# Linear attention and a gated spatial unit on one core: x of the fourth batch turned by TensorE, variance offset and mean subtraction moved from VectorE into GpSimd's root and the normalization, and a new order table

## The chip, the cores and the metric

The kernel runs on one core of one Trainium2 chip. Its time is the device time of one execution in microseconds (us). A core has five engines with a queue each: TensorE (PE in the profile, its weight loads PEld), VectorE (DVE), ScalarE (ACT), GpSimd (POOL) and SyncE (SP), which here issues DMAs only. An instruction waits for semaphores of other engines at the head of its engine's queue, and whatever stands behind it waits too.

## The reference

Eight batches, eight heads, 576 tokens, head width 64. Attention is linear, with 128 random features:

```python
proj = np.einsum('bhsd,df->bhsf', x, w_phi)
proj = proj - np.max(np.abs(proj), axis=-1, keepdims=True)
phi  = np.concatenate([np.exp(proj), np.exp(-proj)], axis=-1)      # for q and for k
kv   = np.einsum('bhsf,bhsd->bhfd', k_p, v);  z = np.sum(k_p, axis=2)
attn = np.einsum('bhsf,bhfd->bhsd', q_p, kv) / (np.einsum('bhsf,bhf->bhs', q_p, z)[..., None] + 1e-06)
```

Its result, heads side by side, is x (8 x 576 x 512) of a gated unit:

```python
h = np.maximum(x @ w_in, 0.0);  u, v = h[..., :512], h[..., 512:]
v_n = (v - mu) / np.sqrt(var + 1e-06)                  # mean and variance over the 512
v_s = np.einsum('ts,bsd->btd', w_spatial, v_n) + b_spatial[None, :, None]
out = (u * v_s) @ w_out
```

## The kernel before, in words

Of each batch, 512 tokens are worked as four blocks of 128 (the main part); the last 64 tokens of two batches together make a fifth block (the tail, names with t at the end, one for each pair g of batches). Operands are bf16, sums fp32 in the eight banks of PSUM.

The work is cut into some 1400 small operations, each a Python function with a two or three letter name, and one long string, ORDER, lists them all in the order in which they are issued. A word `kp.0.1:2,3` is operation kp of batch 0, part 1, with buffers (or banks) 2 and 3; `@V`, `@A`, `@P`, `@S` names the engine of an operation that several engines can do: VectorE, ScalarE, GpSimd, SyncE. So the table decides three things: the order within each engine's queue, which engine does a copy or a normalization, and which buffer is used. Semaphores between engines follow from the buffers. An operation that is listed early on one engine can still run long before or after its neighbours in the list that are on other engines.

The stages of a batch b, with names:

- lk, lq: loads of k and q (from GpSimd's queue, with conversion to bf16); lv: v (from SP's queue). For the first batch's k, lkf and ckf load in quarters and convert on an engine.
- xk, xq: k and q turned by a transposing DMA on SP's queue; tk, tq with copies tkc, tqc: the same by TensorE and a copy, for the first batches.
- kp: projection of keys, km: largest magnitude (VectorE, L539), ke: the two exponentials (ScalarE, L543), kee and kem: exponentials of the maxima (L548). vs: v times these (L599), vsz: the column that gives z, vst and vstz: the same of the tail (L614). kv: the products of keys and values (TensorE, L634, and L636 with the tail's keys), kvc: copy of the result.
- qp, qm, qs, qt, qc: the same for queries, with the maxima split into two bf16 numbers (qs, L651 and L652), turned (qt) and copied (qc); qf: features with the maxima subtracted by matmuls (L660, L664), qe: exponentials (L669); qn: product with kv (L718), qr and qx: reciprocal (L724) and x (L731).
- x turned, into xT: by TensorE (tx, L801) and a copy (txc) for batches 0, 1 and 2, by a transposing DMA on SP's queue (xx, L794) for batches 3 to 7.
- vm: product with the v half of w_in (L833), vr: relu into vr; vb and va: statistics and aggregate on VectorE (L861, L867), which leave mean and variance in mv.
- vx and vy: add 1e-6 to the variance (L838), and negate the mean (L841), both in place on VectorE; vw: the root, GpSimd's power with exponent -0.5 (L844) into rs; vn: normalization, (vr + mv) * rs (L847), on VectorE or GpSimd. vbt, vat, vxt, vyt, vwt, vnt are the same for a tail.
- um and ur: the u half (L931) and its relu; sm: the spatial product (L946 with vn, L948 with the tail's vnt; smt, L992 and L994, gives the tail's tokens), sg: times u (L955); om: product with w_out (L960; omt, L1006, of the tail), oc: copy into ob, od: store.

The warm operations are matmuls on zeros (L334) in the gaps of the first stretch, whose results nobody reads. mv, rs and the banks are taken from small sets of buffers (six mv, five rs, three xT, three ld, four v).

The lines around the change:

```python
def prepare(mv):
    nc.vector.tensor_scalar(out=mv[:, :, 1], in0=mv[:, :, 1], scalar1=1e-6, scalar2=None, op0=ALU.add)
def negate(mv):
    nc.vector.tensor_scalar(out=mv[:, :, 0], in0=mv[:, :, 0], scalar1=-1.0, scalar2=None, op0=ALU.mult)
def root(rs, mv, r=slice(0, P)):
    nc.gpsimd.tensor_tensor(out=rs, in0=mv, in1=neghalf[r, 0:rs.shape[1]], op=ALU.pow)
def normalize(e, out_, in_, mv, rs):
    ENG[e].tensor_scalar(out=out_, in0=in_, scalar1=mv, scalar2=rs, op0=ALU.add, op1=ALU.mult)
```

Of the kernel before, what the change touches and what calls it, by code (L numbers as in the profile page):

```python
# [27 lines left out]
vs.0.1.1@P qt.0.1:3 qp.1.0.1:0,1 kem.0.2 vsz.0.2:3@P qc.0.1:1@V tqc.1.0.1:5@V vst.0.0.1@V vst.0.0.0@P vs.0.0.1@P
lv.0.1:1@S qst.0:2@P tq.1.0.0:4 qe.0.0.1.0:1 tqc.1.0.0@V qe.0.0.1.1 qf.0.1.1:2,3 qm.1.0.1:3 qe.0.1.1.1:2 kv.0.1:5
qe.0.1.1.0 qp.1.1.0:6,7 qm.1.1.0:0 vs.0.2.0@V kv.0.0:4 qf.0.1.0:0,1 vs.0.2.1@P qp.1.1.1:2,3 kvc.0.0:0@A kvc.0.1@A  # L30
qtt.0:4 qn.0.0.0:6,7 qct.0:2@A qe.0.1.0.0:3 qm.1.1.1 tk.1.0.1:4 kv.0.2:5 tkc.1.0.1:6@V qp.1.0.0:2,3 vs.0.3.0@P
kvc.0.2@A vs.0.3.1@P vst.0.1.0@P qe.0.1.0.1 tk.1.0.0:4 vst.0.1.1@P qr.0.0.0:0 kv.0.3:5 qx.0.0.0:0 qm.1.0.0 tkc.1.0.0@V
kvc.0.3@A lkt.1:0@S qft.0:6,7 lqt.1:1@S ckt.1:0@P qs.1.0:2@P qn.0.0.1:0,1 qr.0.0.1:1 qn.0.1.0:2,3 qx.0.0.1 qr.0.1.0:2
lv.1.0:2@S kp.1.1:4,5 qet.0.1:4 qx.0.1.0:1 qet.0.0 qn.0.1.1:0,1 qr.0.1.1:0 qnt.0.0:6,7 qx.0.1.1 tk.1.1.1:2 lv.1.1:3@S
ke.1.1.1:4 lk.2:2 qrt.0.0:1 tx.0.2:3 tq.2.0.0:0 tkc.1.1.1:0@V tx.0.1:1 tk.1.1.0:2 qxt.0.0:0 ke.1.1.0 txc.0.2:0@A
kp.1.0:6,7 tx.0.0:3 km.1.1:3 txc.0.1@A tkc.1.1.0@V tx.0.3:1 qt.1.0:4 txc.0.0@V qc.1.0:0@V vm.0.2:5 txc.0.3@V
tqc.2.0.0:1@V ke.1.0.0:1 ke.1.0.1 txt.0.0:4 qs.1.1:2@P vr.0.2:0@A lbs:0@S kp.1.3:2,3 ke.1.3.1:0 lq.3:1 kp.1.2:0,1
# [20 lines left out]
vb.1.2:0 qp.3.0.0:4,5 qe.2.0.0.0:4 sm.0.1:0 sm.0.2:1 qe.2.1.1.1:0 qe.2.1.1.0 qm.3.0.0 vs.2.1.0@P qe.2.0.0.1 sg.0.1
kp.3.0:4,5 qf.2.0.1:6,7 sg.0.2 va.1.0:2 vs.2.2.0@P qe.2.0.1.0:2 qp.3.1.1:0,1 zmhl.0@V km.3.0:0 kv.2.2:2 qm.3.1.1
vs.2.3.1:3@P vs.2.3.0@P xq.4.0:0@S vs.2.1.1@P qe.2.0.1.1 lv.4.0:3@S vsz.2.3@P lv.4.1:2@S vst.1.1.0@P um.1.0:3  # L60
qp.4.0.0:6,7 vsz.2.0:2@P kvc.2.2:2@A kp.3.1:0,1 ke.3.0.1:0 um.1.3:2 qs.3.1:2@P ur.1.0@V vs.2.0.0@P qst.1:0@P
xq.4.1:1@S ke.3.0.0 sm.0.0:3 qtt.1:4 km.3.1 qm.4.0.0:1 qct.1:0@V kv.2.1:5 ur.1.3@A ke.3.1.1:3 kee.3.0:0 qt.3.1:2
xk.4.0:3@S kv.2.3:4 sg.0.0 kp.3.3:6,7 qc.3.1:2@V kvc.2.1@A vbt.0.1:2 ke.3.1.0 kvc.2.3@A kp.3.2:2,3 om.0.0:5 km.3.3:2
ke.3.2.1:2 vs.2.0.1@P oc.0.0:0@V qs.3.0:0@P vsz.3.1:1@P ke.3.3.1:1 om.0.2:4 qt.3.0:0 vb.1.1:1 qc.3.0:1@V km.3.2
ke.3.3.0 kv.2.0:1 kvc.2.0@A om.0.3:5 oc.0.3:1@V vsz.3.0:0@P xk.4.1:5@S smt.0.0:0 oc.0.2:2@A sgt.0.0 qp.4.1.0:6,7
qf.3.0.0:4,5 qm.4.1.0:2 qn.2.0.1:0,1 qr.2.0.1:1 qx.2.0.1:1 ke.3.2.0 qn.2.1.0:2,3 qe.3.0.0.1:3 lk.5:0 qe.3.0.0.0
vs.3.0.1@P vst.1.1.1@P vs.3.1.0@P qft.1:6,7 vs.3.0.0@P qr.2.1.0:2 qn.2.0.0:0,1 lq.5:1 qn.2.1.1:4,5 qx.2.1.0:0
qet.1.0:2 om.0.1:2 qet.1.1 qr.2.0.0:0 ckt.2:0@P va.1.1 qx.2.0.0 od.0.0@S qr.2.1.1:1 vat.0.1:3 tx.2.1:3 lv.3.1:0@S
txc.2.1:2@A va.1.2 kee.3.1:1 oc.0.1:3@A vxt.0.1@V lk.6:2 vwt.0.1:2@P qp.4.1.1:0,1 qf.3.0.1:6,7 vyt.0.1@V qx.2.1.1
qm.4.1.1 qp.4.0.1:4,5 xk.5.0:4@S kv.3.0:3 tx.2.2:2 qe.3.0.1.0:1 tkt.2:0 vm.2.1:1 va.1.3 qm.4.0.1 qe.3.0.1.1 vnt.0.1@P  # L70
vr.2.1:2@A qf.3.1.0:4,5 kvc.3.0:0@V tktc.2:0@V vy.1.2@V kp.4.0:6,7 vx.1.2@V txc.2.2@V xk.5.1:2@S tx.2.3:3 vs.3.1.1@P
qe.3.1.0.0:4 kv.3.1:0 ke.4.0.1:4 tx.2.0:1 txc.2.3@V vb.2.1:1 kvc.3.1@A vm.2.2:2 qs.4.0:2@P qe.3.1.0.1 vsz.3.2:3@P
vw.1.2:3@P txc.2.0@V vm.2.0:3 vn.1.0:2@P va.2.1:4 km.4.0:3 vn.1.3@P vn.1.1@V qf.3.1.1:0,1 vn.1.2@P vr.2.2:1@A
kp.4.2:4,5 vs.3.2.1@P vsz.3.3:2@P sm.1.0:2 lvt.2:0@S vr.2.0:4@V sm.1.2:3 od.0.3@S km.4.2:1 vs.3.2.0@P vb.2.2:2
ke.4.0.0 qe.3.1.1.0:0 um.2.1:6 sg.1.0 smt.0.1:7 ke.4.2.1:0 sg.1.2 ke.4.2.0 qe.3.1.1.1 ur.2.1:0@V kp.4.1:2,3 vs.3.3.0@P
lqt.2:1@S kp.4.3:4,5 qs.4.1:0@P vb.2.0:0 vs.3.3.1@P sgt.0.1 kv.3.3:6 km.4.3 ke.4.1.1:3 kv.3.2:0 kvc.3.3@A kvc.3.2@A
# [75 lines left out]
def kernel(  # L152
# [684 lines left out]
    def prepare(mv):  # L837
        nc.vector.tensor_scalar(out=mv[:, :, 1], in0=mv[:, :, 1], scalar1=1e-6, scalar2=None, op0=ALU.add)  # L838

    def negate(mv):  # L840
        nc.vector.tensor_scalar(out=mv[:, :, 0], in0=mv[:, :, 0], scalar1=-1.0, scalar2=None, op0=ALU.mult)  # L841
# [214 lines left out]
```

## Time and profile before

| | |
|---|---|
| median of three runs | 260.94 us (259.86 to 262.88) |
| the profiled execution | 262.09 us, its span 260.3 us |
| TensorE busy | 243.9 us, 94% of the span |
| VectorE busy | 227.4 us, 87% |
| ScalarE busy | 193.2 us, 74% |
| GpSimd busy | 149.7 us, 58% |
| DMA | 40.79 MB moved, mean 157 GB/s |

How to read the profile's lines. A row of the windows holds a stretch of the span in us, its length, and for PE, PEld, DVE, ACT and POOL the busy time and, in brackets, the number of instructions; then the granted clock of TensorE as a share of full speed, the busy share of the DMA engines and the GB/s moved. A row of the timeline begins with start and duration in us, then the engine, the line of the code, the operation, what it writes and reads by the program's names with the shapes, and the count of instructions drawn together; in square brackets stands how long the engine was idle before it and what ended that. A row of the groups has the line, the engine and the operation, then busy time and mean ns of one instruction, then the idle time before the group's instructions and what ended most of it. The chain of waits is followed back from the last instruction: each step goes to what released it. A matmul's record reaches from its start to its modelled end, and one starts before the last has ended, so a busy TensorE need not be a full one.

### The profile page before, as it was taken

The numbers are of one execution on the slowest core, as the hardware profiler recorded it, in microseconds if no ns is written. First come the engines' busy times: TensorE is split into PE (matmuls) and PEld (weight loads), VectorE is DVE, ScalarE is ACT, GpSimd is POOL, SyncE is SP. The second block draws the span as 40 slices with busy tenths as digits, with TensorE's granted clock in tenths as the row PEclk, the third lists the DMA queues.
The fourth block names the chain that finished last, engine by engine and source line by source line (L and its number), as shares of the span: only waits on it lengthen the run. The fifth ranks groups of instructions, "written<-read, shape, count | busy, mean of one in ns | idle before, by whom it ended". The sixth has DMA issues, their size and how long they took to land.

```text
span 260.3 us, 8002 instructions
## 1 busy us (share of the span) xinstructions
PE 243.9 (94%) x3250; PEld 150.4 (58%) x3287; DVE 227.4 (87%) x427; ACT 193.2 (74%) x298; POOL 149.7 (58%) x235
## 2 busy tenths in 40 slices
...
GB/s 147 245 234 192 220 221 183 183 236 218 157 156 199 207 113 117 186 179 236 127 183 183 118 226 189 159 144 167 0 83 22 63 86 79 78 123 43 168 195 201
DMA packets 77767, 40.79 MB, mean 157 GB/s; under 512 B 46754, under 2 KB 72994, under 8 KB 77732
## 3 DMA queue, kind: packets, MB, share of 16 engines
...
q14 instruction: 10, 0.08, 0.2%
...
## 4 chain that ended last, share of the span: by engine, by line
PE 53%; DVE 26%; issue 9%; DMA 6%; ACT 2%; POOL 2%; POOLq 0%; DVEq 0%; ACTq 0%
PE banks L833 8%; PE banks L931 6%; PE banks L946 6%; DVE mq L539 6%; PE banks L634 5%; PE banks L960 5%; PE banks L534 5%; DVE mk L539 4%; PE banks L718 3%; DVE x L731 3%; DMA xT<-x 3%; PE banks L660 2%; DVE uT L955 2%; PE banks L664 2%; DMA T<-ld 2%
## 5 line engine op out<-in xcount | busy, mean ns | idle before, releaser
L669 ACT ACTIVATE qf<-banks 128x1024 bf16<-128x1024 f32 x72 | 70.2, 1035 | 6.8 <-PE banks L664 6.2
L599 POOL TENSOR_TENSOR vs<-v,em 128x512 bf16<-128x512 f32 x59 | 62.9, 1080 | 9.7 <-ACT em L548 9.4
L543 ACT ACTIVATE kf<-banks 128x1024 bf16<-128x1024 f32 x64 | 63.8, 1038 | 5.6 <-PE banks L534 4.6
L539 DVE TENSOR_REDUCE mk<-banks 128x8 f32<-128x1024 f32 x36 | 43.5, 1212 | 1.5 <-ACT kf L543 1.0
L539 DVE TENSOR_REDUCE mq<-banks 128x8 f32<-128x1024 f32 x36 | 43.1, 1211 | 0.5 <-PE banks L534 0.4
L844 POOL TENSOR_TENSOR rs<-mv,neghalf 128x4 f32<-128x4 f32 (+2 forms) x13 | 11.0, 844 | 52.6 <-DVE mv L838 50.5
L833 PE MATMUL banks<-w_v,xT 128*128 128x512 bf16 x115 | 30.6, 379 | 3.0 <-DMA xT<-x 2.2
L946 PE MATMUL banks<-w_spT,vn 128*128 128x512 bf16 x118 | 31.9, 379 | 0.5
L931 PE MATMUL banks<-xT,w_u 128*128 128x512 bf16 x128 | 32.3, 380 | 0.1
L960 PE MATMUL banks<-w_out,uT 128*128 128x512 bf16 x118 | 30.9, 379 | 0.6 <-issue 0.2
L255 ACT COPY ob<-banks 128x512 f32<-128x512 f32 x24 | 14.0, 589 | 21.6 <-PE banks L960 10.2
L534 PE MATMUL banks<-wphi,T 64*128 64x128 bf16 x512 | 23.7, 217 | 1.6 <-DVE mq L539 0.9
L955 DVE TENSOR_TENSOR uT<-banks,uT 128x512 bf16<-128x512 f32 x32 | 21.1, 678 | 4.1 <-PE banks L948 2.9
L634 PE MATMUL banks<-vs,kf 128*128 128x66 bf16 x512 | 23.9, 194 | 0.6 <-DVE vs L599 0.4
L634 PEld LDWEIGHTS <-kf 128*128 128x128 bf16 x512 | 21.5, 97 | 3.4 <-issue 0.5
L731 DVE TENSOR_TENSOR x<-banks,rc 128x512 bf16<-128x512 f32 x32 | 22.0, 686 | 0.8
L718 PEld LDWEIGHTS <-qf 128*128 128x128 bf16 x512 | 19.1, 97 | 4.5 <-issue 0.2
L861 DVE BATCH_NORM_STATS2 st<-vr 128x6 f32<-128x512 bf16 x32 | 21.3, 678 | 0.1
L636 PE MATMUL banks<-vst,kft 128*128 128x66 bf16 x128 | 21.1, 192 | 0.0
L534 PEld LDWEIGHTS <-T 64*128 64x128 bf16 x512 | 15.8, 94 | 8.9 <-issue 6.0
L718 PE MATMUL banks<-kv,qf 128*128 128x66 bf16 x512 | 20.4, 193 | 0.3 <-DVE x L731 0.3
L261 ACT ACTIVATE vr<-banks 128x512 bf16<-128x512 f32 (+1 forms) x21 | 12.8, 608 | 9.8 <-PE banks L833 9.5
...
## 6 DMA issues: line engine op xcount, KB each, us to landing
...
```

Of the source, the lines that this page charges most:

```text
L534: nc.tensor.matmul(out=bank(banks[y])[:, n * F:(n + 1) * F], lhsT=xT[halves[y], n, :], rhs=wphi[halves[y], :], start=True, stop=True)
L539: nc.vector.tensor_reduce(out=out_, in_=pp.rearrange("p y (n f) -> p y n f", f=F), axis=AX.X, op=ALU.max, apply_absolute_value=True)
L543: nc.scalar.activation(out=kf[:, s].rearrange("p y n f -> p y (n f)"), in_=pp, func=AF.Exp, bias=0.0, scale=(1.0, -1.0)[s])
L599: ENG[e].tensor_tensor(out=at["vs", (b, j)][:, s, :, 0:D], in0=at["v", (b, j // 2)][:, (j % 2) * n:(j % 2 + 1) * n, :], in1=at["em", (b, j ...
L634: nc.tensor.matmul(out=pv[:, hh, s, :], lhsT=kf[:, s, c % 2, 2 * hh + c // 2, :], rhs=w[:, s, NB * hh + c, :], start=(c == 0), stop=False)
L669: nc.scalar.activation(out=at["qf", u][:, s].rearrange("p y n t -> p y (n t)"), in_=at["pq", u], func=AF.Exp, bias=0.0, scale=(1.0, -1.0)[s])
L718: nc.tensor.matmul(out=at["pn", u][:, y, n, :], lhsT=f[:, s, y, n, :], rhs=at["kv", b][:, hg * HH + n, s, :], start=(s == 0), stop=(s == 1))
L731: nc.vector.tensor_tensor(out=at["x", (b, cc)][:, :, hg * HH:(hg + 1) * HH, :], in0=at["pn", u][:, :, :, 0:D], in1=at["rc", u].to_broadcas ...
L833: nc.tensor.matmul(out=bank(place)[r], lhsT=lhs[:, kc, r], rhs=w_v[:, kc, :], start=(kc == 0), stop=(kc == KC - 1))
L931: nc.tensor.matmul(out=bank(place).rearrange("p (c t) -> p c t", c=NB), lhsT=w_u[:, kc, dc * P:(dc + 1) * P], rhs=at["xT", b][:, :, kc, :] ...
L946: nc.tensor.matmul(out=bank(place), lhsT=at["vn", b][:, c, cs], rhs=w_spT[:, c, 0:T0], start=(c == 0), stop=False)
L960: nc.tensor.matmul(out=bank(place), lhsT=at["uT", b][:, dc, c * P:(c + 1) * P], rhs=w_out[:, dc, :], start=(dc == 0), stop=(dc == KC - 1))
```

## The change

Three things change together.

1. The operations vx, vy, vxt and vyt are gone, 26 instructions on VectorE. The root gets an addition of 1e-6 to the variance in place, on GpSimd, ahead of its power; the normalization subtracts the mean instead of adding its negative.

2. x of batch 3 is turned by TensorE (tx.3.0 to tx.3.3, four transposes each, with copies txc.3.0 on ScalarE and txc.3.1 to txc.3.3 on VectorE) instead of by xx.3.0 and xx.3.1, two transposing DMAs.

3. The table is a new one throughout: order, engines and buffers. Some counts of operations by engine, before and after: vs on VectorE 5 and 2 (GpSimd 59 and 62); vst on VectorE 2 and 0; vn on VectorE 8 and 4, on GpSimd 24 and 28; vnt on VectorE 2 and 0; ur on VectorE 14 and 9, on ScalarE 18 and 23; vr on VectorE 15 and 17; kvc on VectorE 11 and 17, on ScalarE 21 and 15; qc and qct on VectorE 16 and 7, on ScalarE 4 and 13. One of the first batch's four key conversions moves from VectorE to GpSimd, and one constant's two copies (zvnt.0) from VectorE to ScalarE. The matmuls on zeros grow from 29 to 33. The first loads are queued differently: of the four key quarters of batch 0, two are issued from SP's and two from ScalarE's queue as before, but all four ahead of any tail load, and the load of batch 1's q (lq.1) follows the first q loads directly on GpSimd's queue.

The core of the diff:

```diff
-    def prepare(mv):
-        nc.vector.tensor_scalar(out=mv[:, :, 1], in0=mv[:, :, 1], scalar1=1e-6, scalar2=None, op0=ALU.add)
-
-    def negate(mv):
-        nc.vector.tensor_scalar(out=mv[:, :, 0], in0=mv[:, :, 0], scalar1=-1.0, scalar2=None, op0=ALU.mult)
-
     def root(rs, mv, r=slice(0, P)):
+        nc.gpsimd.tensor_scalar(out=mv, in0=mv, scalar1=1e-6, scalar2=None, op0=ALU.add)
         nc.gpsimd.tensor_tensor(out=rs, in0=mv, in1=neghalf[r, 0:rs.shape[1]], op=ALU.pow)
 
     def normalize(e, out_, in_, mv, rs):
-        ENG[e].tensor_scalar(out=out_, in0=in_, scalar1=mv, scalar2=rs, op0=ALU.add, op1=ALU.mult)
+        ENG[e].tensor_scalar(out=out_, in0=in_, scalar1=mv, scalar2=rs, op0=ALU.subtract, op1=ALU.mult)
...
-    @op
-    def vx(e, b, i):
-        prepare(at["mv", b][:, spans[i]])
-
-    @op
-    def vy(e, b, i):
-        negate(at["mv", b][:, spans[i]])
...
-    @op
-    def vxt(e, g, i):
-        prepare(at["mv", ("t", g, i)][rows[i], 0:1, :])
-
-    @op
-    def vyt(e, g, i):
-        negate(at["mv", ("t", g, i)][rows[i], 0:1, :])
```

And the first lines of the table, before and after:

```diff
-zsp@V zvst.0@V cident@P lkf.1:0@A zmhl.2@V csel@V lkf.0:1@S zvnt.0@V ckf.1:0@V ckf.0@V lq0.4.4:1 lphi@A cphi@V
-warm.10:0 tk.0.0.1:0 lkf.3:2@A tkc.0.0.1:0@V lq0.0.4 tk.0.0.0:1 tkc.0.0.0@A ckf.3@P lkt.0:0@S csel2@V warm.1:2
-kp.0.1:2,3 warm.1:4 kp.0.0:4,5 ke.0.0.0:0 km.0.1:0 warm.8:6 tq.0.1.0:0 ke.0.1.1:1 km.0.0 tk.0.1.1:1 lkf.2:3@S lq.1:2
+zsp@V lkf.1:0@S zvst.0@V zmhl.2@V cident@P ckf.1:0@V lphi@A lq0.0.4:1 lq0.4.4 lkf.3:1@A lkf.2:2@A zvnt.0@A warm.8:0
+tk.0.0.1:0 csel@V csel2@V cphi@V tkc.0.0.1:0@A warm.4:1 kp.0.1:2,3 lkf.0:3@S lq.1:2 ckf.3@P warm.5:1 tk.0.1.1:0
+km.0.1:0 ckf.0@P kem.0.1:0 warm.1:1 tk.0.0.0:1 ckf.2@P tkc.0.1.1:1@V tkc.0.0.0@V kp.0.3:4,5 warm.1:6 kp.0.0:6,7
```

More of the change, by code (lines that the diff above doesn't have):

```diff
@@ L28 @@
[L28 to L37, printed above, removed]
@@ L58 @@
[L58 to L67, printed above, removed]
@@ L68 @@
[L68 to L76, printed above, removed]
-qt.4.0:1 qc.4.0:0@V vm.2.3:7 xq.5.0:6@S qnt.1.2:0,1 sm.1.1:6 km.4.1 ke.4.3.1:1 ke.4.3.0 ke.4.1.0 vr.2.3:3@A
@@ new lines @@
+kvc.0.0@A qn.0.1.0:6,7 qm.1.1.1 qr.0.1.0:0 ke.1.1.1:4 qx.0.1.0:0 qct.0:2@A ke.1.1.0 vs.0.3.0@P vs.0.3.1@P qs.1.1:2@P
+kv.0.2:3 kvc.0.2@A qft.0:0,1 km.1.1:3 qet.0.0:4 kv.0.3:2 qt.1.1:3 lv.2.1:0@S qc.1.1:0@A kvc.0.3@V qn.0.0.0:6,7
+qr.0.0.0:1 qx.0.0.0:1 qet.0.1 kp.1.0:4,5 lqt.1:1@S vst.0.1.0@P qn.0.1.1:2,3 ke.1.0.0:2 qr.0.1.1:2 qx.0.1.1
+qn.0.0.1:0,1 qr.0.0.1:0 qnt.0.0:6,7 ke.1.0.1 tx.0.3:2 qx.0.0.1 qrt.0.0:1 qs.1.0:2@P txc.0.3:0@A qt.1.0:3 qc.1.0:1@V
+qxt.0.0:0 tq.2.0.0:0 km.1.0 tq.2.1.1:1 tqc.2.0.0:1@A tq.2.0.1:3 kp.1.2:6,7 tqc.2.0.1@A tx.0.0:0 txt.0.0:2 txtc.0.0:0@V
@@ new lines @@
+sm.0.2:6 qf.2.1.0:2,3 qf.2.0.0:0,1 sg.0.2 vs.2.1.1@P ur.1.2:2@A vb.1.1:0 vs.2.3.1:3@P qp.4.1.0:4,5 qe.2.1.0.0:1
+qe.2.0.0.0:2 vsz.2.3@P qe.2.1.0.1 qe.2.0.0.1 vs.2.3.0@P qm.4.1.0:3 qs.3.1:1@P vsz.2.0@P lq.5:1 vs.2.2.1:2@P kv.2.1:6
+va.1.1 vb.1.3:2 sm.0.1:7 sg.0.1 kv.2.3:4 kvc.2.1:2@V kvc.2.3@A vb.1.0:3 um.1.1:5 vs.2.2.0@P qp.3.0.0:2,3 ur.1.1@A
+qm.3.0.0 vst.1.1.1@P xq.4.1:3@S kp.3.1:6,7 lqt.2:0@S kp.3.0:0,1 ke.3.1.1:0 km.3.0:1 lv.5.1:2@S ke.3.1.0 km.3.1
+vs.2.0.0@P vsz.2.2@P um.1.0:4 ur.1.0@A sm.0.3:5 kv.2.0:2 kvc.2.0@V kv.2.2:4 ke.3.0.0:1 va.1.3 kp.3.3:6,7 lkt.2:1@S
@@ new lines @@
+qp.4.0.1:0,1 oc.0.1:2@A um.1.3:3 qe.3.0.1.0:3 km.3.2 qm.4.0.1:2 tx.2.0:2 vst.1.1.0@P tx.2.1:4 qtt.1:5 qp.4.1.1:0,1
+qe.3.0.1.1 qct.1:0@V kee.3.1:2 ur.1.3@A vsz.3.0@P txc.2.1@V vn.1.0@P qft.1:6,7 vn.1.1@P vsz.3.1@P txc.2.0@A vn.1.2@P
+qm.4.1.1 qet.1.1:1 qet.1.0 qp.4.0.0:4,5 qm.4.0.0 smt.0.0:3 vm.2.2:2 sgt.0.0 qf.3.0.0:0,1 vsz.3.2:1@P kp.4.0:4,5
+vr.2.2:3@V km.4.0:2 vm.2.1:3 vr.2.1:1@V tx.2.3:2 qe.3.0.0.1:0 qe.3.0.0.0 sm.1.1:6 txc.2.3@V sg.1.1 qs.4.1:1@P
+ke.4.0.1:4 kv.3.0:7 qf.3.1.0:0,1 kvc.3.0:0@V lv.3.1:1@S vs.3.2.1@P kp.4.2:2,3 kp.4.1:6,7 ke.4.0.0 qe.3.1.0.0:4
@@ new lines @@
+tqtc.2:0@A vs.4.1.0:2@P qr.3.0.1:0 ur.2.2@A vs.4.2.0@P lk.6:1 qx.3.0.1 va.2.2 vst.2.0.1:0@P kp.5.0:0,1 kp.5.1:2,3
+vstz.2@P ke.5.1.1:3 vmt.1.2:6 vst.2.0.0@P vrt.1.2:0@A tx.3.2:7 qm.5.0.1 vw.2.2:4@P tx.3.3:4 kv.4.0:5 vn.2.2:0@P
+om.1.2:6 km.5.0:0 ke.5.1.0 txc.3.3:0@V txc.3.2@V vbt.1.2:1 kvc.4.0:1@A xq.6.0:5@S od.0.2@S oc.1.2:0@V tx.3.1:7
+ke.5.0.0:4 vsz.4.1@P xq.6.1:4@S vn.2.0@P om.1.3:4 ke.5.0.1 vat.1.2:5 km.5.1 vs.4.1.1@P vwt.1.2:1@P tx.3.0:5 qs.5.0:1@P
+vm.3.2:6 ckt.3:0@P qpt.2:0,1 lq.7:2 txc.3.0@A oc.1.3:1@A qf.4.0.1:2,3 qp.5.1.1:4,5 txc.3.1@V qe.4.0.1.1:4 qe.4.0.1.0
@@ new lines @@
+um.3.0:7 qmt.2:3 vr.3.2:3@V qt.5.0:0 vm.3.0:1 qm.5.1.1 vsz.4.3@P kee.5.0:2 vr.3.0:2@A qc.5.0:2@A kv.4.1:6 vst.2.1.1@P
+vn.2.1@P kvc.4.1@A kp.5.2:2,3 ur.3.0:1@V qp.6.1.0:4,5 qm.6.1.0:2 kp.5.3:0,1 ke.5.3.1:1 km.5.2:2 ke.5.3.0 km.5.3
+um.3.3:6 vs.4.2.1@P kv.4.2:7 um.2.1:4 kvc.4.2@V vm.3.3:5 ur.3.3@A kv.4.3:6 xk.6.1:3@S ke.5.2.0:2 vn.2.3@P odt.0@S
+lv.6.1:3@S xk.6.0:1@S vr.3.3:1@A kee.5.1:0 qn.4.0.0:0,1 qr.4.0.0:1 vs.5.0.0:3@P kvc.4.3@A vst.2.1.0@P um.3.2:5
+qf.4.1.0:6,7 vb.3.3:0 ke.5.2.1 qx.4.0.0:1 qp.6.1.1:2,3 qm.6.1.1 qn.4.0.1:0,1 qr.4.0.1:2 qx.4.0.1 vnt.1.2:0@P ur.2.1@A
```

189 lines of the change are left out of this document (96 added, 93 removed).

## The prediction

> **What bounds the kernel now.** I read the windows first, because the two halves of this program have different limits, then the timeline around the one stretch where every engine pauses, then the groups of lines for the durations. The windows give, per stretch, its length and then the busy time of PE, PEld, DVE, ACT and POOL.
>
> ```profile
> span 260.3 us, 8002 instructions
> 0.00:20.00 20.00, 15.59 (x158) 8.58 (x160) 16.82 (x28) 13.91 (x24) 11.59 (x27) 0.96 1.08 209
> 20.00:40.00 20.00, 18.63 (x338) 13.85 (x336) 19.23 (x36) 18.20 (x29) 14.82 (x22) 0.95 1.22 206
> 40.00:100.00 60.00, 59.17 (x913) 39.03 (x923) 58.99 (x112) 58.46 (x92) 49.01 (x77) 1.00 1.17 183
> 100.00:125.00 25.00, 21.35 (x308) 12.81 (x311) 22.03 (x39) 19.60 (x31) 19.18 (x29) 1.00 1.25 193
> 125.00:200.00 75.00, 73.59 (x1047) 46.20 (x1058) 70.82 (x128) 64.20 (x98) 45.74 (x72) 1.00 0.65 131
> 200.00:256.40 56.40, 55.60 (x498) 29.95 (x502) 39.51 (x90) 18.30 (x30) 9.38 (x11) 1.00 0.42 109
> ```
>
> From 40 to 100 us VectorE and ScalarE are both full (58.99 and 58.46 of 60): two bounds side by side, so relief of one alone is worth little there. From 125 to 200 us ScalarE has 10.8 us to spare and VectorE only 4.2, so VectorE is the tighter of the two. From 200 us on only TensorE is full. Its matmuls overlap, so "busy" is no measure of a dense queue; the last product is: 20 matmuls of 512 columns in 4.48 us, about 0.22 us each, with no gap, and the rows ahead of it join without gaps too.
>
> ```profile
> 249.91 1.03 PE L931 MATMUL banks<-xT,w_u 128*128 128x512 bf16 x4
> 250.78 1.03 PE L946 MATMUL banks<-w_spT,vn 128*128 128x512 bf16 x4
> 251.86 4.48 PE L960 MATMUL banks<-w_out,uT 128*128 128x512 bf16 x20
> ```
>
> So after 200 us an engine other than TensorE gains nothing; all that can be won is won before.
>
> One place loses time on all engines. The chain of waits holds the transposing DMA of batch 3 for 7.40 us, and the timeline shows three engines idle at its end: TensorE 2.23 us, VectorE 2.24, ScalarE 3.01.
>
> ```profile
> 114.53 7.40 DMA xT<-x
> 121.97 1.04 PE L833 MATMUL banks<-w_v,xT 128*128 128x512 bf16 x4 [2.23 <-DMA xT<-x]
> 123.12 0.69 DVE L263 TENSOR_SCALAR vr<-banks 128x512 bf16<-128x512 f32 x1 [2.24 <-PE banks L833]
> 123.38 1.94 ACT L543 ACTIVATE kf<-banks 128x1024 bf16<-128x1024 f32 x2 [3.01 <-PE banks L534]
> ```
>
> **The change part by part.** These rows price it (busy time, then mean ns of one).
>
> ```profile
> L838 DVE TENSOR_SCALAR mv<-mv 128x4 f32<-128x4 f32 (+2 forms) x13 | 1.9, 149 | 0.1
> L841 DVE TENSOR_SCALAR mv<-mv 128x4 f32<-128x4 f32 (+2 forms) x13 | 2.8, 215 | 0.1
> L599 POOL TENSOR_TENSOR vs<-v,em 128x512 bf16<-128x512 f32 x59 | 62.9, 1080 | 9.7 <-ACT em L548 9.4
> L599 DVE TENSOR_TENSOR vs<-v,em 128x512 bf16<-128x512 f32 x5 | 5.1, 1028 | 0.0
> L614 POOL TENSOR_TENSOR vst<-vt,em 64x512 bf16<-64x512 f32 x14 | 14.4, 1038 | 2.4 <-ACT em L548 1.9
> L847 POOL TENSOR_SCALAR vn<-vr,mv,rs 128x512 bf16<-128x512 bf16 x24 | 19.1, 804 | 0.6
> L847 DVE TENSOR_SCALAR vn<-vr,mv,rs 128x512 bf16<-128x512 bf16 x8 | 4.1, 525 | 1.4 <-POOL rs L844 1.4
> L847 DVE TENSOR_SCALAR vnt<-vr,mv,rs 64x512 bf16<-64x512 bf16 x4 | 1.6, 408 | 0.6 <-POOL rs L844 0.6
> L652 POOL TENSOR_TENSOR mhl<-mq,mhl 128x16 bf16<-128x16 f32 (+1 forms) x20 | 4.3, 215 | 1.6
> L844 POOL TENSOR_TENSOR rs<-mv,neghalf 128x4 f32<-128x4 f32 (+2 forms) x13 | 11.0, 844 | 52.6 <-DVE mv L838 50.5
> L263 DVE TENSOR_SCALAR uT<-banks 128x512 bf16<-128x512 f32 x14 | 9.5, 681 | 1.0 <-PE banks L931 1.0
> L257 DVE CAST kv<-banks 128x264 bf16<-128x264 f32 x11 | 4.6, 416 | 0.9 <-PE banks L636 0.9
> L261 ACT ACTIVATE uT<-banks 128x512 bf16<-128x512 f32 x18 | 11.0, 612 | 7.4 <-PE banks L931 7.4
> L255 ACT CAST kv<-banks 128x264 bf16<-128x264 f32 x21 | 8.1, 393 | 2.1 <-PE banks L636 1.9
> L543 ACT ACTIVATE kf<-banks 128x1024 bf16<-128x1024 f32 x64 | 63.8, 1038 | 5.6 <-PE banks L534 4.6
> 58.96 0.83 PE banks L801 x12
> ```
>
> Offset and negation: 13 times 0.149 and 13 times 0.215 leave VectorE, 4.7 us. GpSimd gets 13 additions on at most 128x4 numbers; no row shows that operation, the nearest small ones are 0.215 (L652) and, above, the power at 0.844, so 2.8 us, with bounds of 2.8 and 11.0. The normalization's subtraction is costed as the addition it replaces (0.804 on GpSimd), with the slower two-operand product (1.080) as the other bound, 0.3 us more for each of 28.
>
> The new table moves much more. Counting each operation's engine in the two tables: 3 vs, 2 vst, 4 vn and 2 vnt (two instructions each) go from VectorE to GpSimd, 3.1 + 1.9 + 2.1 + 1.6 = 8.7 us off VectorE. Between VectorE and ScalarE, five ur (0.681) and nine qc and qct go to ScalarE, six kvc (0.416) and two vr come back; netted (on ScalarE a ur is 0.612, a kvc 0.393) and with the turned blocks of the start counted the same way, VectorE loses some 1.6 us more and ScalarE gains 3.8. So VectorE loses 15 us in all, ScalarE gains 4 and GpSimd some 15 (11.6 for the products and normalizations, 2.8, and one conversion).
>
> Transposes of batch 3: 16 more on TensorE, by the L801 row 0.07 us each, 1.1 us, and four copies (three VectorE, one ScalarE); two DMAs leave SP's queue, behind which stood loads and other transposes.
>
> What lies on the path, stretch by stretch:
>
> - To 50 us: ahead of the last x of batch 0 the new table puts about 3 us more on ScalarE (three more key exponentials at 1.038; a constant's copies and two mT against two kvc about cancel), and ahead of batch 1's last key product four more GpSimd operations (a vs, a vst, a conversion, a load's issue), 3.6 us. In the trace these key products follow directly on GpSimd's products, but GpSimd sat 3.94 us idle shortly before, so most is covered. Against that, the key loads of the start are issued earlier, the fourth from ScalarE's queue instead of behind a tail's load. I take +0.9; bounds -1.5 and +3.5.
> - 50 to 100: VectorE has 3 to 4 us less at equal progress, ScalarE the same, so only the idle time that one makes for the other can go. ScalarE's is 1.5 of 60 us and VectorE's 1.0. I take -0.8; bounds 0 and -2.0.
> - 100 to 125: the wait on xT goes, -2.2. What is late next are the kp and qp of the following batches, also behind DMAs; bounds 0 and -3.0. The 1.1 us of transposes fill such gaps.
> - 125 to 200: up to 4 us less VectorE work at equal progress, in a stretch with 4.2 us of VectorE idle and 10.8 of ScalarE. I take -1.5; bounds 0 and -3.3.
> - From 200: nothing to gain. 158 matmuls of 512 columns stand behind the last x of batch 7 instead of 136, so 22 times 0.22, 4.8 us, of cover more: the tail is safer, not shorter. The last four vn are now all GpSimd's, 0.804 each, just ahead of the tail product that waited 0.21 us before; +0.6, bounds 0 and +1.5.
>
> ```profile
> 7.35 1.94 ACT L543 ACTIVATE kf<-banks 128x1024 bf16<-128x1024 f32 x2 [0.85 <-PE banks L534]
> 36.62 0.19 POOL L651 CAST mhl<-mq 128x16 bf16<-128x16 f32 x1 [3.94 <-PE banks L656]
> 44.80 4.03 POOL L599 TENSOR_TENSOR vs<-v,em 128x512 bf16<-128x512 f32 x4
> 46.22 0.30 PE L634 MATMUL banks<-vs,kf 128*128 128x66 bf16 x4
> 243.52 0.26 PE L992 MATMUL banks<-w_spT,vn 128*128 128x64 bf16 x3 [0.21 <-POOL vn L847]
> ```
>
> Sum: 0.9 - 0.8 - 2.2 - 1.5 + 0.6 = -3.0. The profiled execution took 262.09 us (span 260.3), which gives 259.1; the median of the runs is 260.94, 1.15 lower, so 257.9 on that scale.
>
> **The rivals.**
>
> 1. *ScalarE holds the pace.* It is as full as VectorE from 40 to 100 us and gets no relief; batch 3's wait turns into the next wait on a DMA or a bank. For it: 58.46 of 60. Against: its 5.4 idle us between 100 and 125, and 10.8 after, which a relieved VectorE can fill. The gains shrink to about -1 and the start costs its +0.9: 260.8, no change.
>
> 2. *GpSimd and VectorE cannot work side by side*, so that work handed from one to the other buys nothing. The trace has signs: a negation of 0.157 us median took 0.939 once while GpSimd ran, a vn on VectorE 0.811 against 0.413.
>
> ```profile
> L841 DVE TENSOR_SCALAR mv<-mv x13: 143/157/939, 59.3 to 240.3; 128x4 f32<-128x4 f32 x8, 128x1 f32<-128x1 f32 x3, 64x1 f32<-64x1 f32 x2
> L847 DVE TENSOR_SCALAR vn<-vr,mv,rs x8: 403/413/811, 99.2 to 242.0; 128x512 bf16<-128x512 bf16 x8
> ```
>
> The -0.8 and -1.5 fall away, -0.7 is left: 260.2. Against: each is a single excess, and VectorE's big groups read PSUM. The Trainium skill's page Perfetto Trace Analysis, section Optimizing Scalar/DVE Operations, says that the two share an SBUF read port, so that shifting work between them might not help; by that rule the time is this rival's 260.2. The trace agrees only in those two maxima.
>
> 3. *Slower: GpSimd becomes the bound in batches 1 to 3.* Ahead of the first key projection of batch 4 the new table gives it four vn, two vs, a vst and a root more (3.2 + 2.2 + 1.0 + 0.8, four additions 0.8, and about -0.7 of loads and conversions): 7.3 us. Before, it idled 11 us between 40 and 100, but waiting for data (em, mv), and its queue is in order: a vs behind a late root is late too. If none of that idle time can be filled, the front loses 7.3 and the -0.8 goes: 0.9 + 7.3 - 2.2 - 1.5 + 0.6 = +5.1, 266.0. It decides for slower, by over 2.6, once about 4.8 of the 7.3 stay uncovered; the dearer subtraction (eight vn, 2.2 us) and additions would bring it nearer. Against: a root now waits for the aggregation alone, not for two VectorE instructions, one of which kept it 2.0 us.
>
> ```profile
> 92.35 0.58 POOL L844 TENSOR_TENSOR rs<-mv,neghalf 64x1 f32<-64x1 f32 x1 [2.04 <-DVE mv L841]
> ```
>
> 4. *More than forecast*: -1.5 at the start, -2.0, -2.6, -2.4 and no tail cost, -8.5: 252.4.
>
> **How the numbers follow.** Forecast 0.42, rival 1 0.20, rival 2 0.05, rival 3 0.25, rival 4 0.08. A measurement of this kernel can tell about 1% (2.6 us) from no change. The forecast at 257.9 lies just past that bound (258.3): of its 0.42 I put 0.30 below it and 0.12 within. Rivals 1 and 2 are within 1% but for 0.02 slower; rival 3 is 0.24 slower and 0.01 within; rival 4 faster. Faster 0.38, same 0.36, slower 0.26. The range, 252.8 to 266.0, leaves out about half of rivals 3 and 4, 0.17. The forecast's own range is 255.5 to 260.5.
>
> **What would show it.** Right: VectorE near 212 us busy, GpSimd near 165, ScalarE near 197; no product with w_v of batch 3 waiting on a DMA; from the last x on, TensorE dense and about 34 us long. Wrong: key products or tail products waiting on GpSimd in batches 1 to 3 (rival 3), its vn well over 0.8 us, or VectorE idle rising while ScalarE stays full (rival 1). A start whose first exponentials come clearly later than at 7.35 us would break the first term.

## The result, and the profile after

The changed kernel takes 298.63 us (median of four runs, 296.32 to 299.53) against 260.55 for the kernel before: slower, ratio 1.129 with a 95% interval of 1.1124 to 1.1455. A fifth run took 292.92. (The ratios in this document leave disturbed runs out, here three of these five, so the loss by the ratio is some 34 us, not the 38 between the medians.) The forecast was 257.9, its range ended at 266.0. The profiled execution took 296.32 us.

The head of its page (PEclk is TensorE's granted clock in 40 equal slices of the span, in tenths of full speed), and the shares of its chain of waits by engine:

```profile
span 294.5 us, 8022 instructions
PE 254.2 (86%) x3267; PEld 153.9 (52%) x3307; DVE 216.1 (73%) x382; ACT 197.3 (67%) x307; POOL 209.9 (71%) x262
PEclk9999999997799889999889999998799999999598
PE 40%; POOL 32%; DVE 13%; DMA 5%; issue 4%; ACT 2%; SPq 1%; POOLq 1%; DVEq 0%; ACTq 0%
```

The chain of the kernel before, for comparison:

```profile
PE 53%; DVE 26%; issue 9%; DMA 6%; ACT 2%; POOL 2%; POOLq 0%; DVEq 0%; ACTq 0%
```

VectorE (216.1) and ScalarE (197.3) came out near the forecast (212 and 197). GpSimd did not: 209.9 us busy, where 165 was forecast and 149.7 was before. Its share of the chain went from 2% to 32%. The reason stands in one row of the groups, and in the normalization's own durations (min/median/max in ns):

```profile
L840 POOL TENSOR_SCALAR vn<-vr,mv,rs 128x512 bf16<-128x512 bf16 x28 | 57.9, 2075 | 1.0
L836 POOL TENSOR_SCALAR mv<-mv 128x4 f32<-128x4 f32 (+2 forms) x13 | 3.4, 265 | 30.0 <-DVE mv L860 25.1
```

```profile
L840 POOL TENSOR_SCALAR vn<-vr,mv,rs x28: 2062/2077/2087, 57.0 to 272.2; 128x512 bf16<-128x512 bf16 x28
L840 POOL TENSOR_SCALAR vnt<-vr,mv,rs x8: 2067/2080/2092, 61.7 to 257.1; 64x512 bf16<-64x512 bf16 x8
L840 DVE TENSOR_SCALAR vn<-vr,mv,rs x4: 344/405/412, 171.5 to 254.5; 128x512 bf16<-128x512 bf16 x4
```

On GpSimd one normalization takes 2.08 us where it took 0.804 (the mean; the median was 0.766). The spread is 25 ns over the whole run, so it is not a matter of what runs beside it; and on VectorE the subtracting expression takes 0.405, as the adding one did before (0.413). The tail's vnt, with half the partitions, takes as long as vn.

The timeline shows what a slow normalization does to an in-order queue, GpSimd first, TensorE then:

```profile
61.67 2.09 POOL L840 TENSOR_SCALAR vnt<-vr,mv,rs 64x512 bf16<-64x512 bf16 x1
63.75 4.12 POOL L840 TENSOR_SCALAR vn<-vr,mv,rs 128x512 bf16<-128x512 bf16 x2
67.85 1.03 POOL L597 TENSOR_TENSOR vs<-v,em 128x512 bf16<-128x512 f32 x1
68.87 2.07 POOL L840 TENSOR_SCALAR vn<-vr,mv,rs 128x512 bf16<-128x512 bf16 x1
```

```profile
67.27 1.04 PE L923 MATMUL banks<-w_spT,vn 128*128 128x512 bf16 x3
71.00 0.61 PE L923 MATMUL banks<-w_spT,vn 128*128 128x512 bf16 x1 [2.68 <-POOL vn L840]
```

The spatial product (L923) issues three matmuls and stands 2.68 us at its fourth until the last vn is there, and all else on TensorE stands behind it. A vs, which the key products need, waits in GpSimd's queue behind three normalizations. TensorE's waits, largest first (us in total, how often, the longest):

```profile
PE banks L923 <- POOL vn L840: 9.3, 5, 3.1
PE banks L632 <- POOL vs L597: 5.4, 4, 2.7
PE banks L969 <- POOL vn L840: 4.8, 3, 1.9
PE banks L654 <- POOL mhl L650: 4.1, 3, 2.9
PE banks L632 <- POOL vs L255: 3.0, 1, 3.0
```

All five end with GpSimd: products waiting for a normalization (L923, L969), for v times the key's factors and for the column that gives z (the two rows of L632), for the split maxima (L654); 26.6 us in all. Before, the five largest were 2.2, 1.6, 1.5, 0.9 and 0.9 us, none on GpSimd. The windows:

```profile
40.00:100.00 60.00, 54.62 (x766) 34.28 (x772) 52.05 (x90) 52.43 (x82) 52.42 (x66) 0.94 1.01 161
125.00:200.00 75.00, 67.96 (x979) 42.55 (x990) 61.04 (x106) 59.72 (x95) 65.13 (x83) 0.98 0.77 147
```

From 40 to 100 us VectorE and ScalarE, 58.99 and 58.46 of 60 before, are at 52: they starve. The granted clock falls to 0.94 there, where it was 1.00; TensorE's record is 254.2 us busy against some 246 in the kernels below that do the same matmuls at nearly full clock.

### The profile page after: what moved, and what is told of

The parts are those of the page before. It is cut to its first block, busy times and chain, and to the rows that moved or that the text cites. A ratio compares the mean times of both kernels' runs of the same rounds, so it can differ in the third digit from the quotient of the medians.

```text
span 294.5 us, 8022 instructions
## 1 busy us (share of the span) xinstructions
PE 254.2 (86%) x3267; PEld 153.9 (52%) x3307; DVE 216.1 (73%) x382; ACT 197.3 (67%) x307; POOL 209.9 (71%) x262
## 4 chain that ended last, share of the span: by engine, by line
PE 40%; POOL 32%; DVE 13%; DMA 5%; issue 4%; ACT 2%; SPq 1%; POOLq 1%; DVEq 0%; ACTq 0%
POOL vn L840 13%; POOL vs L597 7%; PE banks L831 6%; PE banks L923 6%; PE banks L937 6%; DMA tf<-in_q_dram 5%; PE banks L908 5%; POOL vnt L840 4%; PE banks L632 3%; DVE mq L537 3%; POOL rs L837 3%; PE banks L716 2%; PE banks L532 2%; DVE st L854 2%; PE banks L925 2%
## 5 line engine op out<-in xcount | busy, mean ns | idle before, releaser
L840 POOL TENSOR_SCALAR vn<-vr,mv,rs 128x512 bf16<-128x512 bf16 x28 | 57.9, 2075 | 1.0
L923 PE MATMUL banks<-w_spT,vn 128*128 128x512 bf16 x116 | 33.3, 388 | 10.8 <-POOL vn L840 9.3
L908 PE MATMUL banks<-xT,w_u 128*128 128x512 bf16 x128 | 34.9, 403 | 0.0
L831 PE MATMUL banks<-w_v,xT 128*128 128x512 bf16 x113 | 32.1, 395 | 1.1 <-issue 0.4
L937 PE MATMUL banks<-w_out,uT 128*128 128x512 bf16 x120 | 32.3, 394 | 0.5 <-issue 0.2
L632 PE MATMUL banks<-vs,kf 128*128 128x66 bf16 x512 | 25.1, 196 | 8.5 <-POOL vs L597 5.4
L932 DVE TENSOR_TENSOR uT<-banks,uT 128x512 bf16<-128x512 f32 x32 | 21.7, 681 | 14.0 <-PE banks L925 13.9
L632 PEld LDWEIGHTS <-kf 128*128 128x128 bf16 x512 | 23.2, 99 | 14.4 <-issue 9.6
L259 ACT ACTIVATE uT<-banks 128x512 bf16<-128x512 f32 x23 | 14.0, 607 | 20.0 <-PE banks L908 19.9
L836 POOL TENSOR_SCALAR mv<-mv 128x4 f32<-128x4 f32 (+2 forms) x13 | 3.4, 265 | 30.0 <-DVE mv L860 25.1
L923 PEld LDWEIGHTS <-vn 128*128 128x128 bf16 x128 | 11.6, 98 | 23.6 <-POOL vn L840 12.0
L259 ACT ACTIVATE vr<-banks 128x512 bf16<-128x512 f32 (+1 forms) x19 | 11.4, 601 | 17.1 <-PE banks L831 10.9
```

What stands on the lines that cost most here:

```text
L632: nc.tensor.matmul(out=pv[:, hh, s, :], lhsT=kf[:, s, c % 2, 2 * hh + c // 2, :], rhs=w[:, s, NB * hh + c, :], start=(c == 0), stop=False)
L831: nc.tensor.matmul(out=bank(place)[r], lhsT=lhs[:, kc, r], rhs=w_v[:, kc, :], start=(kc == 0), stop=(kc == KC - 1))
L908: nc.tensor.matmul(out=bank(place).rearrange("p (c t) -> p c t", c=NB), lhsT=w_u[:, kc, dc * P:(dc + 1) * P], rhs=at["xT", b][:, :, kc, :] ...
L923: nc.tensor.matmul(out=bank(place), lhsT=at["vn", b][:, c, cs], rhs=w_spT[:, c, 0:T0], start=(c == 0), stop=False)
L937: nc.tensor.matmul(out=bank(place), lhsT=at["uT", b][:, dc, c * P:(c + 1) * P], rhs=w_out[:, dc, :], start=(dc == 0), stop=(dc == KC - 1))
```

## The experiments

Theory S: the loss comes from the form of the normalization, subtract and then multiply, which GpSimd works at 2.08 us instead of 0.8; the rest of the change is worth about what was forecast. Rival T: the table loads GpSimd too much (the forecast's rival 3), whatever the form. Rival C: the additions and the root on GpSimd, or the TensorE turn, do it.

**The addition form back, all else as changed.** The mean is negated again, in one kernel by a small GpSimd instruction ahead of the root (the diff), in the other by VectorE (`nc.vector` in its place).

```diff
+    def negate(mv):
+        nc.gpsimd.tensor_scalar(out=mv, in0=mv, scalar1=-1.0, scalar2=None, op0=ALU.mult)
...
-        ENG[e].tensor_scalar(out=out_, in0=in_, scalar1=mv, scalar2=rs, op0=ALU.subtract, op1=ALU.mult)
+        ENG[e].tensor_scalar(out=out_, in0=in_, scalar1=mv, scalar2=rs, op0=ALU.add, op1=ALU.mult)
...
+        negate(at["mv", b][:, spans[i], 0])
...
```

> The changed kernel with its table, transposes and root kept; only the normalization adds again, of a mean that a small GpSimd instruction negates ahead of the root. Theory S (the subtracting normalization on GpSimd is slow: 36 instructions at 2.08 us instead of 0.77, 47 us more of GpSimd, and the waits behind it are the whole loss): normalization back at 0.77, GpSimd near 167 busy, the time where the forecast without it stood, 256 to 262. Rival R (the new table overloads GpSimd or runs late by itself, with the product work that it moved there): 270 or more, with key products still waiting for GpSimd.

> As e1_add_neg_pool, but the 13 negations run on VectorE. Theory S: within 1% of e1_add_neg_pool, since 13 times 0.16 on VectorE and 13 times 0.24 on GpSimd are both small. Rival R: also 270 or more.

Measured: 260.67 us (10 runs; ratio to before 0.9963, 0.9908 to 1.0018) and 259.83 (10 runs; 0.9981, 0.9937 to 1.0024). From the trace of the first, with its negation (L836) and its offset (L839):

```profile
L836 POOL TENSOR_SCALAR mv<-mv x13: 242/253/581, 55.7 to 236.3; 128x4 f32<-128x4 f32 x8, 128x1 f32<-128x1 f32 x3, 64x1 f32<-64x1 f32 x2
L839 POOL TENSOR_SCALAR mv<-mv x13: 218/228/237, 56.0 to 236.7; 128x4 f32<-128x4 f32 x8, 128x1 f32<-128x1 f32 x3, 64x1 f32<-64x1 f32 x2
L843 POOL TENSOR_SCALAR vn<-vr,mv,rs x28: 760/772/932, 57.5 to 240.4; 128x512 bf16<-128x512 bf16 x28
L843 POOL TENSOR_SCALAR vnt<-vr,mv,rs x8: 764/771/778, 61.0 to 226.1; 64x512 bf16<-64x512 bf16 x8
```

The loss is gone with one word of code and 13 more instructions on GpSimd. The form costs 36 times 1.31, 47 us of GpSimd (the busy times agree: 209.9 against 166.1, which includes 3.6 for the negations), and some 34 of these 47 came through to the end. T and C are out as causes by themselves: table, additions and turn are all still there. What is left of the change can't be told from no change.

**The slow form alone, in the table of before.** The operations that negate the mean (vy, vyt) are taken out of the table (the diff shows one of the 13), and the normalization subtracts.

```diff
-        ENG[e].tensor_scalar(out=out_, in0=in_, scalar1=mv, scalar2=rs, op0=ALU.add, op1=ALU.mult)
+        ENG[e].tensor_scalar(out=out_, in0=in_, scalar1=mv, scalar2=rs, op0=ALU.subtract, op1=ALU.mult)
...
-va.7.2 vy.7.2@V smt.3.0:2
+va.7.2 smt.3.0:2
...
```

> The kernel before with its own table, where only the normalization subtracts and the 13 negations are left out. Theory S: 28 GpSimd instructions go from 0.77 to 2.08, 37 us more GpSimd; 282 to 300, TensorE waiting for vn and vs, and TensorE's clock halved in some of the gaps. Rival R: the table is the old one, so 258 to 266.

Measured: 285.64 us (4 runs), ratio 1.0928 (1.0828 to 1.1029).

```profile
L847 POOL TENSOR_SCALAR vn<-vr,mv,rs 128x512 bf16<-128x512 bf16 x24 | 50.7, 2117 | 0.6
L847 POOL TENSOR_SCALAR vnt<-vr,mv,rs 64x512 bf16<-64x512 bf16 x4 | 8.3, 2076 | 0.2
```

GpSimd is 186.7 us busy, 37.0 more than before, and some 24 of them, by the ratio, reach the end. With 28 normalizations on GpSimd the price is thus some seven tenths of the 34 us with 36. The new table has eight more of the slow instructions on GpSimd; whether the loss goes by their number alone, two different tables can't show.

**The subtraction, but all of it on VectorE,** in the changed kernel: each `vn` and `vnt` of the table marked `@P` becomes `@V`.

```diff
-vnt.0.0:0@P vn.0.0@P zmhl.1@V
+vnt.0.0:0@V vn.0.0@V zmhl.1@V
```

> The changed kernel with all 37 normalizations on VectorE, still subtracting. Theory S: subtraction costs nothing on VectorE (0.41 each), GpSimd loses 75 us (near 135 busy), VectorE gains 15 (near 231, about as much as before the change): 258 to 266. Rival R, whose trouble is the table's order and its products on GpSimd: 270 or more.

Measured: 269.04 us (4 runs), ratio 1.0338 (1.0224 to 1.0452).

```profile
L840 DVE TENSOR_SCALAR vn<-vr,mv,rs x32: 344/407/1290, 56.7 to 248.7; 128x512 bf16<-128x512 bf16 x32
```

Most of the loss goes, so it is GpSimd's handling of the form, and not the arithmetic. But it is 3 us above the expected range: VectorE is 12 us busier than after (228.4 against 216.1), TensorE waits 3.5 us for its normalizations, and the time is 8 to 9 us above the two kernels with the addition form, which have 36 of these normalizations on GpSimd.

**Which forms are slow.** In the table of before, the normalization of batch 1 subtracts and multiplies (L851), of batch 2 multiplies and adds (L853), of batch 3 multiplies and subtracts (L855), of batch 4 only subtracts (L857), of batch 5 only adds (L859), without the product with rs. Batches 1 to 5 thus aren't normalized as the reference has it, and only the durations are of interest.

```diff
+    def forms(e, b, out_, in_, mv, rs):
+        if b == 1:
+            ENG[e].tensor_scalar(out=out_, in0=in_, scalar1=mv, scalar2=rs, op0=ALU.subtract, op1=ALU.mult)
+        elif b == 2:
+            ENG[e].tensor_scalar(out=out_, in0=in_, scalar1=rs, scalar2=mv, op0=ALU.mult, op1=ALU.add)
+        elif b == 3:
+            ENG[e].tensor_scalar(out=out_, in0=in_, scalar1=rs, scalar2=mv, op0=ALU.mult, op1=ALU.subtract)
+        elif b == 4:
+            ENG[e].tensor_scalar(out=out_, in0=in_, scalar1=mv, scalar2=None, op0=ALU.subtract)
+        elif b == 5:
+            ENG[e].tensor_scalar(out=out_, in0=in_, scalar1=mv, scalar2=None, op0=ALU.add)
...
```

> The kernel before, with other forms of the normalization in batches 1 to 5 (1: subtract, multiply; 2: multiply, add; 3: multiply, subtract; 4: subtract alone; 5: add alone), so that those batches normalize otherwise than the reference; only the mean duration of each form on GpSimd is wanted. If the subtraction itself is what is slow there: about 2.08 us for batches 1, 3 and 4, about 0.77 for 2 and 5. If instead add-then-multiply is one fast pair and every other pair is slow: 2.08 for 1, 2 and 3, and single operations fast.

Measured, on GpSimd, in one run (L847 is the form of before, in batches 0, 6 and 7):

```profile
L847 POOL TENSOR_SCALAR vn<-vr,mv,rs x8: 757/766/902, 61.4 to 251.5; 128x512 bf16<-128x512 bf16 x8
L851 POOL TENSOR_SCALAR vn<-vr,mv,rs x3: 2068/2090/2112, 98.1 to 102.3; 128x512 bf16<-128x512 bf16 x3
L853 POOL TENSOR_SCALAR vn<-vr,rs,mv x4: 757/761/765, 125.6 to 138.7; 128x512 bf16<-128x512 bf16 x4
L855 POOL TENSOR_SCALAR vn<-vr,rs,mv x3: 2071/2071/2087, 156.9 to 161.1; 128x512 bf16<-128x512 bf16 x3
L857 POOL TENSOR_SCALAR vn<-vr,mv x3: 1558/1563/2007, 183.8 to 193.1; 128x512 bf16<-128x512 bf16 x3
L859 POOL TENSOR_SCALAR vn<-vr,mv x3: 1553/1559/1894, 212.6 to 216.0; 128x512 bf16<-128x512 bf16 x3
```

The slow thing is not subtraction as such. An addition by itself takes as long as a subtraction by itself (1.56), and both take twice as long as addition and multiplication together (0.766). Fast are the two pairs of addition and multiplication, in either order; a pair with a subtraction in either place takes 2.07 to 2.09. A fused pair of two operations can thus be twice as fast as half of it.

**The variance offset alone,** in the table of before: the addition of 1e-6 goes into GpSimd's root, vx and vxt go, the negation stays on VectorE.

```diff
     def root(rs, mv, r=slice(0, P)):
+        nc.gpsimd.tensor_scalar(out=mv, in0=mv, scalar1=1e-6, scalar2=None, op0=ALU.add)
```

> The kernel before with the variance offset alone moved into GpSimd's root (13 additions there at about 0.24 us, 13 VectorE instructions of 0.149 gone; the negation stays). Theory S with the forecast's prices: 3 us more of GpSimd and 2 us less of VectorE, both small: 259 to 262, no change. A rival that the root's longer chain delays the tail: 263 or more.

Measured: 260.26 us (12 runs), ratio 0.9967 (0.993 to 1.0004). Nothing that can be told from no change.

**The turn of batch 3 by TensorE alone,** in the table of before, first with all four turns in one bank (the diff shows the words of the table that change), then spread over two banks (4 and 5) and away from their users.

```diff
-xx.3.0:0@S
+tx.3.0:4 txc.3.0:0@V tx.3.1:4 txc.3.1@A
...
-xx.3.1@S
+tx.3.2:4 txc.3.2@V tx.3.3:4 txc.3.3@A
```

> The kernel before with x of batch 3 alone turned by TensorE and copied (two copies on VectorE, two on ScalarE), table otherwise kept. The forecast's step: the wait on xT goes, 2.2 us less, 258 to 259. Rival (a wait of TensorE's takes its place, or TensorE's 1.1 us of transposes cost as much): 260 to 262.

> The table of before with x of batch 3 turned by TensorE, as in the run before it, but the turns are spread over two banks (4 and 5) and stand one or more matmul groups away from their copies and from the product with w_v, so that no turn waits for the copy just ahead of it. If the 263.95 of the run with one bank came from its four waits on copies (0.59, 0.68, 0.52 and 0.67 us, 2.5 in all, where the wait on the DMA was 2.23), these go and the time is 260 to 262, before's within a half per cent: then the turn by itself is worth nothing in this order, because its 16 transposes (1.1 us) and four copies take what the wait gave. If the forecast's term of -2.2 holds, 258 to 259. If the loss does not hang on the banks at all, it stays at 263.5 to 264.5.

Measured: 263.95 us (12 runs; ratio 1.0115, 1.0082 to 1.0148) and 263.79 (6 runs; 1.0116, 1.0068 to 1.0165). So the turn alone costs 1.2% in the old order, and it isn't that the four turns share a bank. TensorE's timeline of the second, around the place where the wait on the DMA was:

```profile
115.97 1.04 PE L833 MATMUL banks<-w_v,xTt 128*128 128x512 bf16 x4 [0.66 <-DMA xTt<-xt]
...
121.41 0.40 PE L534 MATMUL banks<-wphi,tT 64*128 64x128 bf16 x8 [1.04 <-ACT qf L669]
...
124.18 0.40 PE L534 MATMUL banks<-wphi,T 64*128 64x128 bf16 x8 [1.18 <-DVE ob L257]
...
126.73 0.29 PE L634 MATMUL banks<-vs,kf 128*128 128x66 bf16 x4
```

The wait of 2.23 us on the DMA is gone; in its place the projections of the following batches (L534) wait 1.04 us for an exponential and 1.18 us for a copy to leave their banks, 2.22 together, and the turns' own matmuls and copies come on top. In the trace of before, the product at 115.97 began at 116.24 and the key products at 126.73 began at 125.45:

```profile
116.24 1.04 PE L833 MATMUL banks<-w_v,xTt 128*128 128x512 bf16 x3 [0.91 <-ACT ob L255]
...
125.45 0.29 PE L634 MATMUL banks<-vs,kf 128*128 128x66 bf16 x4
```

From the one to the other 10.76 us now, 9.21 before: 1.55 longer, where 2.2 less was forecast. That is about what separates these two traced executions (263.62 and 262.09); before's was 1.5 us above its median, so the other half of the 1.2% isn't accounted for.

**The turn undone in the new order.** The kernel with the addition form and VectorE's negation, with batch 3 by DMAs again (the diff shows the words of the table that change); both once more in a second comparison.

```diff
-tx.3.2:7
-tx.3.3:4
+xx.3.1:0@S
...
-txc.3.3:0@V txc.3.2@V
-tx.3.1:7
+xx.3.0@S
...
-tx.3.0:5
-txc.3.0@A
-txc.3.1@V
```

> The new table with the adding normalization and the negation on VectorE (as e1v_add_neg_vector), but x of batch 3 turned by two DMAs again in the places of the transposes. The forecast's step: about 2 us slower than e1v_add_neg_vector's 259.8, 261 to 263. Rival (in this order the DMAs are hidden and TensorE is 1.1 us lighter): 258 to 260.

> The kernel with the addition form, the negation on VectorE and the rest of the change, a second time, beside the next one on one chip: 259.5 to 260.5 as before, if the rest of the change is worth less than 0.5 per cent. If it is worth the forecast's 1.2 per cent, 257 to 258.5.

> The same with x of batch 3 turned by DMAs, a second time. If the wait on the transposing DMA costs in this order what its trace shows (3.0 us of TensorE idle) less the 1.1 us of transposes saved, it is 1.5 to 3 us above the run before it: 261.5 to 263.5. The first time showed 265.98, 6 above; if that holds there is more in it than the wait.

Measured: 265.98 us (6 runs; ratio to before 1.0129, 1.0054 to 1.0204), and the second time 264.30 (6 runs; 1.0132, 1.0071 to 1.0193) beside 260.42 for the kernel with the turn (12 runs; 0.9974, 0.9932 to 1.0015). In the trace of the second:

```profile
126.89 1.05 PE L913 MATMUL banks<-xT,w_u 128*128 128x512 bf16 x4 [2.44 <-DMA xT<-x]
```

In the new order the turn is worth 3.9 us: the wait is back without it, now ahead of the product with w_u (L913). It is more than the 1.5 to 3 expected; the rest isn't accounted for.

## Why the prediction was wrong, point by point

**The step that failed** is the price of the normalization: "The normalization's subtraction is costed as the addition it replaces (0.804 on GpSimd), with the slower two-operand product (1.080) as the other bound, 0.3 us more for each of 28". Measured: 1.31 more for each of 36 (the 28 and the eight of the tail), 47 us. Taking the addition's price assumed that the operation doesn't matter, only the shape, and put the term at nothing in the sum; and the upper bound was no bound at all, since it came from another kind of instruction (two tensors as operands). No row of the trace of before shows a GpSimd pair with a subtraction, so a bound from the trace had to be a wide one; the power (0.844 for at most 128x4 numbers, where a subtraction of 128x16 took 0.215) was a sign in that trace that the operation matters on this engine. The Trainium skill's page GPSIMD Engine Reference, section 3.1 (Elementwise — side-by-side cycle accounting), has 769 ns measured for 512 elements as a best case of a tight loop. The pairs of addition and multiplication, 0.761 to 0.772 us in the median, take as long; at 1.56 and 2.08 the other forms are far from that case.

**Rival 3 named the engine, not the cause or the size.** GpSimd did become the bound, by its queue and by key products and spatial products that wait for it, from batch 0 on. Of its signs, the vn well over 0.8 us appeared as said. The other came elsewhere: key products waited for GpSimd in batch 0 (30.6 us) and in batches 4, 5 and 7 (146.0, 160.9 and 232.6 us), while in the time of batches 1 to 3 it was the spatial products that did (71.0 and 110.2 us). Its 266.0 came from four more normalizations and their neighbours at the old price. With the addition form this table shows no such bound: TensorE's largest waits on GpSimd in the 260.67 us kernel are 1.9, 1.2 and 0.7 us.

**The additions:** 0.215 each was estimated, 0.239 was the median after. Right, and hidden.

**The rest of the sum was -3.0 us (-1.2%); it measured -0.4% with GpSimd's negation, -0.2% and -0.3% with VectorE's,** with intervals (down to 0.9908, 0.9937 and 0.9932) that leave the forecast out. The negation stays in these kernels, so one small part of the -3.0 isn't in them, on VectorE 13 instructions of 0.158 us. Where the gain went is seen if the span is cut at the start of the last x of batch 7. Windows of before (cut at 223.98), then of the kernel with the addition form and VectorE's negation (cut at 215.84):

```profile
0.00:223.98 223.98, 211.93 (x3072) 135.50 (x3107) 205.68 (x380) 184.61 (x283) 143.83 (x228) 0.99 0.92 159
223.98:260.30 36.32, 31.99 (x180) 14.93 (x181) 21.72 (x47) 8.62 (x15) 5.90 (x7) 1.00 0.45 145
```

```profile
0.00:215.84 215.84, 207.99 (x3070) 131.85 (x3071) 194.81 (x349) 186.65 (x290) 152.82 (x247) 1.00 0.91 162
215.84:258.20 42.36, 37.86 (x239) 18.40 (x237) 21.75 (x47) 9.86 (x17) 10.19 (x15) 0.97 0.41 125
```

Up to the last x the gain was 8.1 us (7.3 and 6.2 in the two other traces with the addition form), and VectorE has 10.9 us less to do there. But this trace of before is of an execution 1.5 us above the median. In the trace of the kernel with the offset alone moved, which takes as long as before, the last x begins at 221.8 us; measured from there the gain is 6.0 us (5.2 and 4.0), still above the forecast's 3.6. And the rest is 6.0 us longer, and TensorE has 5.9 us more to do in it. The forecast saw the 22 more matmuls of 512 columns that stand behind the last x and called them cover: "the tail is safer, not shorter". They are TensorE's own work, put off. In the part after the last x TensorE waits for nothing in that trace, and a matmul of 512 columns takes the same 379 ns as before, so the longer tail is the moved work. TensorE as a whole was the bound that the forecast looked past: VectorE and ScalarE were as full as it from 40 to 100 us, but over the span TensorE's work does not shrink (243.9 us busy before, 245.9 now, the trace of before lacking some 37 records), and only its idle time can be won. That is 16.4 us in this trace of before and 13.9 in the one with the offset alone moved (the missing records count as idle in both), and 12.4, 13.6 and 13.9 in the three with the addition form: hardly less, so hardly any span was won. No run moved the matmuls of the tail back by themselves.

**The terms in turn.** *100 to 125, the wait on xT, -2.2:* in the new order the turn is worth this and more (3.9), in the old order it costs 3; the term holds only with the order that the table gives it. "What is late next are the kp and qp of the following batches" was right in the old order, but it took the whole of the wait, and the turns' own work came on top: a bound of no gain was too good, since the turn could cost time. *50 to 100 and 125 to 200, -2.3 together:* VectorE's relief came, and was spent as said. *From 200, +0.6:* missed by 5.4, the backlog; its sign, some 34 us from the last x on, came out as 42.4 with the addition form and as 49.7 in the changed kernel. *To 50 us, +0.9:* not separated by a run; in the three traces with the addition form the last key product of batch 1 begins 1.0 to 3.4 us later than before.

**Rival 1** (260.8) and **rival 2** (260.2) gave about the time of the rest of the change, which does not show their reasons. Against rival 2's, that handing work from VectorE to GpSimd buys nothing, stands that with all normalizations on VectorE the time was 8 to 9 us longer than with 36 of them on GpSimd in the addition form. Also, without the turn of batch 3 the new table with the addition form still brings the last x at 219.1 and 219.3 us, 2.5 us or more earlier than the old one. Rival 1's reason was not tested.

**Left open:** how much of the 34 us is TensorE's lower clock (mean 0.95 in the changed kernel). From 71 to 73 and from 204 to 209 us, right behind waits of 2.68 and 3.14 us for a normalization, the granted clock is 0.50. TensorE's busy time is 8.3 us above that of the kernel with the addition form, which bounds the part roughly; no run held the clock up while leaving the waits.
